# Three schedule edits in an attention and mixture-of-experts kernel: a weight load in pieces, conversions in set rounds, one step of the output normalisation a round later

## The chip, the cores and the metric

One Trainium2 chip, one of its cores. The time is device microseconds from launch to end, the median of the runs. The core has a matrix engine (TensorE, PE in the rows; PEld is its weight load), a vector engine (VectorE, DVE), a scalar engine (ScalarE, ACT), a general engine (GpSimd, POOL) and a queue engine (SyncE, SP) that issues the DMAs here. The five run side by side and wait on each other's semaphores; each runs its own instructions in the order in which the program issued them.

## What is computed

```python
def _attn_ref(q, k, v, centroids):           # batch 2, 8 heads, 768 rows, head_dim 64, 16 clusters
    q_assign = argmax(q_n @ c_n.T); k_assign = argmax(k_n @ c_n.T)      # nearest centroid of each row
    scores = scale * q @ k.T
    scores = where(q_assign[:, None] == k_assign[None, :], scores, -1e9)
    attn = exp(scores - max(scores)); attn /= attn.sum() + 1e-9
    return attn @ v
def _moe_ref(x, w_in, w_out):                # x 1536 x 512, w_in 512 x 2048, both weights float64
    r = maximum(x @ w_in, 0.0); return (r * r) @ w_out
def _moe2_ref(x, domain_probs, w1, w2):      # 4 experts, w1 512 x 1024, w2 1024 x 512
    return sum_e p[:, e:e+1] * (maximum(x @ w1[e], 0) @ w2[e])
```

The first mixture takes the attention's output, the second takes the first one's. Products are made from a high and a low half of each operand in the fast 32-bit matrix format.

## The kernel before

**Attention (to about 268 us).** The 16 heads of both batches are taken two at a time: pair j holds heads 2j and 2j+1. A head has six query tiles of 128 rows, so there are NU = 96 tiles and the loop at line 1094 has 96 rounds, g = 0 to 95. Twelve rounds make a pair; I call g modulo 12 the *turn*. Round g issues, in the order of letters in ORDER (one list for even, one for odd g):

- S: score products of tile g+2 (line 580: two products with q1 and k1, then two with q2 and k2, whose lower rows hold the cluster's one-hot code and so the mask), M: its row maximum on DVE (line 589), E: exp of tile g+1 on ACT (line 600);
- T0, T1: transposes of tile g's exponentials (line 613), with a high copy on ACT (H, line 618) and a low rest on DVE (L, line 619); P0, P1: the product with v (lines 627, 629); O: the copy of a finished output block (line 651);
- X1, X2: at most two *slots*, extra PE jobs taken from `slots` and from `nq`, whose evacuations follow at Y1, Y2; R: what is listed in `early` for this round (DMAs, split of v); C: one entry of the list `dq` of small operations; K: one step of a weight conversion (`convert`).

So even rounds run "S T0 X1 M E T1 R Y1 H0 P0 X2 C H1 L0 L1 C K Y2" and odd ones "S X1 E M T0 T1 Y1 H0 C P1 X2 R L0 H1 C L1 O K Y2 C".

**A pair's preparation** (for j > 1 at turns 10 to 7 ahead of its first tile): four transposes `trans_slot` (line 354; ACT copy, then two POOL operations, lines 52 and 363), two `pair_scores` (line 404), two `pair_turn` (line 420, with DVE sums at line 425). The second `pair_turn` empties `dq` and starts the *cluster chain* `pair_ops`: a DVE maximum (459), three POOL operations (449 to 451), four empty entries, a second DVE maximum (460), four POOL operations (454 to 457). In the eight entries the two maxima and the two POOL groups are m1, p1, four Nones, m2, p2; two are issued at once and the rest one for each C. Then `pair_hot` (line 471) transposes the codes, ACT copies them (476), and `hot_rows` issues four small DMAs (488) into rows D to D+C of q2 and k2, which the second half of S needs. `stack` issues the DMAs of q1, k1, q2, k2 (375, 377). The first pair of this kind, j = 1, has its own rounds in START: transposes in rounds 0, 0, 1, 1, `pair_scores` twice in round 3, `pair_turn` twice in round 4, `pair_hot` in round 7.

**Normalising a pair's output** (`norm_slots`): the list `nq` is filled when a pair's last output block is copied (turn 1) and gives one entry for each following round. f1 (turn 2) puts four small DVE operations at the head of `dq` (lines 670 to 673); f2 (turn 5) transposes the reciprocal sums (679) and, in its evacuation, copies them on ACT (683) and adds the output halves with two POOL additions (688); f3 (turns 8 and 9) spreads them (696), multiplies and splits (702 to 716).

**Weights.** Those of the first mixture are float64, loaded as raw words into `raw` (two buffers, `rawp`). `load_w` at line 111 loads half a part in one DMA of 1 MB. Part 0 of chunk 0 (`raw_t[0, 0, half]`) is loaded ahead of the loop (first half) and in round 4 (second half, line 1082). A column block is converted by `split64`: f1, f2, f4, f5, f6 on DVE (lines 160 to 176) in one scratch buffer `cva`, then f3: an ACT copy (182) and a POOL subtraction (184) that reads `cva` again. The four blocks make 24 steps in `cq`; `convert` takes one in every round from 8 on in which `dq` is empty. When `cq` is empty, `load_piece` loads the next weights in rounds with g % 6 = 4, two pieces each.

**The mixtures (268 us to the end)** are PE products with their evacuations (lines 738 to 920). The change doesn't touch them.

Of the kernel before, what the change touches and what calls it, by code (L numbers as in the profile page):

```python
# [8 lines left out]
F32 = mybir.dt.float32  # L9
F32R = mybir.dt.float32r  # L10
I32 = mybir.dt.int32
# [15 lines left out]
WARM = [12, 10, 5, 11, 3, 9]  # L27
START = {'t': [0, 0, 1, 1], 'a': [3, 3, 4, 4, 7], 'stack1': 4, 'stack': 5, 'head': 2, 'gap': 3}
AT = {"gap": 4, "stack1": -11, "stack": -9, "ohd": -7, "splitv": -3, "load": -8,
      "t": [-14, -13, -12, -11], "a": [-10, -10, -9, -8, -5], "conv": 8}  # L30


@with_exitstack
def moe_attention_kernel(
# [13 lines left out]
    nc = tc.nc  # L48

    def round_pool(dst, src):  # L50

        nc.gpsimd.tensor_scalar(dst, src, 1.0, 1.0, op0=ALU.mult, op1=ALU.mult)
# [5 lines left out]
    NTT = S // 128  # L58
    KD = DM // 128
    TB = 512  # L60
    NTB = NT // TB
    FC = 512
# [9 lines left out]
    rawp = ctx.enter_context(tc.tile_pool(name="raw", bufs=2))  # L72
# [25 lines left out]
    wi32 = moe_w_in.bitcast(I32).rearrange("(k p) f -> p k f", p=128)  # L98
    wo32 = moe_w_out.bitcast(I32).rearrange("(k p) f -> p k f", p=128)
    raw_t = {}  # L100
# [10 lines left out]
    def load_w(ci, part, half):  # L111
        r = rawp.tile([128, 2048], F32, tag="raw", name="raw")
        raw_t[ci, part, half] = r
        r = r.bitcast(I32)
        if part == 0:
            f0 = 2 * (ci * FC + half * FC // 2)
            nc.sync.dma_start(
                out=r.rearrange("p (k f) -> p k f", k=KD), in_=wi32[:, :, f0:f0 + FC])
        else:
            f0 = ci * NF + half * NF // 2  # L120
            nc.sync.dma_start(
                out=r.rearrange("p (k f) -> p k f", k=NF // 2), in_=wo32[:, f0:f0 + NF // 2])

    def w_loads(ci):
        return [(ci, part, half) for part in range(2) for half in range(2)]
# [73 lines left out]
    with tc.manual_schedule():  # L199
# [87 lines left out]
        dq = []  # L287
# [57 lines left out]
        def trans_slot(j, nm, half):  # L345

            def f():
                if half == 0:
                    kq[j, nm] = [kq_p.tile([128, S], F32R, tag=nm + x, name=nm + x) for x in "hl"]
                hs = slice(half * HALF, (half + 1) * HALF)  # L350
                hi, lo = kq[j, nm][0][:, hs], kq[j, nm][1][:, hs]
                m = ps_m.tile([128, HALF], F32, tag="m", name="m")
                for t in range(QT):
                    nc.tensor.transpose(
                        m[:, t * 128:(t + 1) * 128],
                        nat["p", j, nm][:, half * QT + t].rearrange("p e d -> p (e d)"), identf)
                mul = scale if nm == "nq" else 1.0

                def evac():
                    x = kq_p.tile([128, HALF], F32, tag="kqf", name="kqf", bufs=3)  # L360
                    nc.scalar.activation(x, m, AF.Copy, scale=mul)
                    round_pool(hi, x)
                    nc.gpsimd.tensor_tensor(lo, x, hi.bitcast(F32), op=ALU.subtract)
                return evac
            return f
# [198 lines left out]
                        m.rearrange("p t n -> p (t n)").bitcast(F32))  # L564

        def pair_slots(j):
            return [trans_slot(j, nm, half) for nm in ("nk", "nq") for half in range(2)]


        late = []  # L570
# [91 lines left out]
        def norm_slots(hp, last=False):  # L662
            st = {}
            def f1():
                sm = sums_t.pop(hp)
                r = sm_p.tile([128, 2, NTT], F32, tag="r", name="r", bufs=1)
                rs = st["rs"] = sm_p.tile([128, NTT, 2, 2], F32R, tag="rs", name="rs", bufs=2)
                rv = r.rearrange("p h t -> p t h")
                dq[:0] = [
                    lambda: nc.vector.tensor_scalar(r, sm, 1e-9, None, op0=ALU.add),  # L670
                    lambda: nc.vector.reciprocal(r, r),
                    lambda: nc.vector.tensor_copy(rs[:, :, :, 0], rv),
                    lambda: nc.vector.tensor_tensor(
                        rs[:, :, :, 1], rv, rs[:, :, :, 0].bitcast(F32), op=ALU.subtract),
                ]

            def f2():
                m = ps_m.tile([NTT * 4, 128], F32R, tag="m", name="m")
                nc.tensor.transpose(m, st["rs"].rearrange("p t h s -> p (t h s)"), identr)

                def evac():
                    rt = st["rt"] = xs_p.tile([NTT * 4, 128], F32R, tag="rt", name="rt")
                    nc.scalar.copy(rt, m.bitcast(F32))
                    if hp in xm_t:
                        xm = xm_t.pop(hp)
                        for c0 in range(0, S, HALF):
                            cs = slice(c0, c0 + HALF)
                            nc.gpsimd.tensor_tensor(  # L688
                                xs_t[hp][:, cs], xs_t[hp][:, cs], xm[:, cs], op=ALU.add)
                return evac  # L690

            def f3(half):
                b, kt = divmod(hp, H // 2)
                m = ps_m.tile([128, HALF], F32, tag="m", name="m")
                for j in range(QT):
                    nc.tensor.matmul(
                        m[:, j * 128:(j + 1) * 128], sel[:, half * QT + j], st["rt"],
                        start=True, stop=True)

                def evac():  # L700
                    rb = xs_p.tile([128, HALF], F32, tag="rb", name="rb")
                    nc.scalar.copy(rb, m)
                    (nc.vector if last else nc.gpsimd).tensor_tensor(
                        rb, rb, xs_t[hp][:, half * HALF:(half + 1) * HALF], op=ALU.mult)
                    c0 = b * S + half * HALF
                    col = c0
                    while col < c0 + HALF:
                        tb, o = divmod(col, TB)
                        n = min(TB - o, c0 + HALF - col)
                        xn = rb[:, col - c0:col - c0 + n]  # L710
                        hi = xh[tb][:, kt, o:o + n]
                        if last:
                            nc.scalar.copy(hi, xn)
                        else:
                            round_pool(hi, xn)
                        (nc.vector if last else nc.gpsimd).tensor_tensor(
                            xl[tb][:, kt, o:o + n], xn, hi.bitcast(F32), op=ALU.subtract)
                        col += n
                return evac

            if last:
                return [f1, f2, lambda: f3(0), lambda: f3(1)]
            return [f1, None, None, f2, None, None, lambda: f3(0), lambda: f3(1)]


        mp = {}
# [206 lines left out]
        for ci in range(NC1):  # L933
            base = 0 if ci == 0 else NF + 2 if ci == 1 else (ci - 1) * per + 2
            for ci, part, half in w_loads(ci):
                if ci == 0 and part == 0:
                    continue
                js = range(2 * half, 2 * half + 2)
                slot = base + (0 if ci == 0 else NF * part)
                if ci > 0:  # L940
                    plan.append((freed[-2], 1, lambda x=(ci, part, half): load_w(*x)))
                for j in js:
                    plan += split_plan(ci, part, j, slot + j)
                freed.append(slot + js[-1] + 1)
# [89 lines left out]
        for e in range(2):  # L1034
            r = slice(D * e, D * e + D)
# [12 lines left out]
        for _ in range(2):  # L1048
            dq.pop(0)()
        nc.sync.dma_start(out=dp, in_=domain_probs.rearrange("(b p t) e -> p b t e", b=B, t=NTT))  # L1050
        load_w(*w_loads(0)[0])


        early, slots = {}, {}

        def at(d, g, f):
            d.setdefault(max(g, 0), []).append(f)
# [11 lines left out]
        for j in range(1, NH // 2):  # L1069
# [9 lines left out]
            if j + 1 < NH // 2:  # L1079
                at(early, u0 + AT["load"], lambda j=j: load_pair(j + 1))  # L1080
        at(slots, START["head"], onehot_slot(1))
        at(early, 4, lambda: load_w(*w_loads(0)[1]))
        cq, lq = [], []
        for j in range(NF):
            cq += [f for fs in split64(0, 0, j, cv_p[0]) for f in fs]
# [2 lines left out]
        nq = []  # L1088
# [5 lines left out]
        for g in range(NU):  # L1094
            par = g % 2
            todo = slots.pop(g, [])
            if nq:
                f = nq.pop(0)
# [28 lines left out]

            def convert():
                if g >= AT["conv"] and cq:
                    if not dq:  # L1130
                        cq.pop(0)()
                elif not cq and g % NTT == 4:
                    for _ in range(2):
                        lq and lq.pop(0)()
# [48 lines left out]

        hp, pr = NH // 2 - 1, NU // 2 - 1
        f1, f2, f3, f4 = norm_slots(hp, last=True)
        f1()
        while dq:
# [64 lines left out]
        for n in range(NN):  # L1252
# [5 lines left out]
            if n:  # L1258
                fills = [[lambda t=t: token_tile(n - 1, t)] for t in range(NTT)] + [[]]
                order = (1, 5, 6, 2, 7, 4, 3)  # L1260
            else:
                fills = [fill[0:1], fill[1:3], fill[3:4], fill[4:5], fill[5:6], fill[6:7], fill[7:8]]
                order = (1, 2, 5, 6, 7, 4, 3)
            for x, i in enumerate(order):
# [35 lines left out]
                if swap:  # L1300
                    r = PROD[i][1]
# [36 lines left out]
```

## Time and profile before

| | |
|---|---|
| runs | 1042.37, 1042.57, 1043.54 us; median 1042.57 us |
| the profiled execution | 1041.03 us, of which 1039.2 us from its first to its last instruction |
| PE busy | 1023.1 us (98%), granted clock 0.998 in the mean |
| DVE, ACT, POOL busy | 677.9, 537.5, 566.0 us |
| attention loop, from the third tile's scores to the last | 19.8 to 268.7 us |

How to read it: with PE at 98% the busy share hides what is lost, because an operation's modelled end includes what it waited for in the pipe. The starts of the score products are a better clock: one group for each round, and twelve rounds for a pair.

### The profile page before, as it was taken

The page shows a single profiled execution, that of the slowest core. Times are in us where ns is not written, and L with a number is a line of the kernel's source. Part 1 is how long each engine was busy: PE and PEld are TensorE (multiplying, and loading weights), DVE is VectorE, ACT ScalarE, POOL GpSimd, SP SyncE. Part 2 cuts the span into 40 slices and gives each one's busy share as a digit, 9 for nine tenths or more (in the row PEclk, how much of TensorE's full clock was granted, in tenths as well). Part 3 has the DMA queues.
Part 4 walks back from the last instruction along what each step waited for, and adds up shares of the span by engine and source line. Part 5 has one row for each costly group of instructions (what it writes and reads, how often), then busy time and mean ns, then how long its engine had stood idle before and what let it go on. Part 6 is the DMA issues. An engine that isn't in the chain of part 4 may idle for free.

```text
span 1039.2 us, 14949 instructions
## 1 busy us (share of the span) xinstructions
PE 1023.1 (98%) x5549; PEld 907.3 (87%) x5549; DVE 677.9 (65%) x1061; ACT 537.5 (52%) x1080; POOL 566.0 (54%) x557
## 2 busy tenths in 40 slices
PE   8899999999999999999999999999999999999998
PEld 7798999999888888888888998998988888898997
DVE  8788888888687773741175555567776555555654
ACT  6788888888755443434443333433444333333331
POOL 4456866674322222235456566567678566576650
PEclk9999999999999999999999999999999999999999
DMA  4755577652023230221012122122123121121101
GB/s 119 179 134 121 130 187 177 148 126 69 1 82 122 82 110 13 81 82 41 1 42 80 43 81 75 47 81 72 51 81 123 60 82 59 63 82 55 67 1 61
DMA packets 72408, 86.05 MB, mean 83 GB/s; under 512 B 26896, under 2 KB 49744, under 8 KB 72336
## 3 DMA queue, kind: packets, MB, share of 16 engines
q1 hardware_dynamic: 72336, 85.11, 28.6%
q8 instruction: 43, 0.70, 0.3%
q14 instruction: 29, 0.24, 0.1%
HBM read 59.83 MB, written 3.15 MB: 61 GB/s over the span
## 4 chain that ended last, share of the span: by engine, by line
PE 85%; DVE 6%; POOL 5%; DMA 1%; issue 1%; ACT 1%; SPq 0%; POOLq 0%; DVEq 0%; ACTq 0%
PE bank L910 25%; PE bank L870 22%; PE bank L763 13%; PE bank L739 4%; PE bank L740 4%; PE bank L738 4%; PE s L580 3%; PE t L613 3%; PE po L627 2%; PE po L629 2%; DVE nb L589 1%; DVE ptl L619 1%; POOL xs L688 1%; DMA k<-nkh 1%; PE m L404 1%
## 5 line engine op out<-in xcount | busy, mean ns | idle before, releaser
L910 PE MATMUL bank<-w1h,ga 128*128 128x512 f32 x768 | 269.9, 393 | 0.0
L920 DVE SCALAR_TENSOR_TENSOR x<-bank,pe_p,x 128x512 f32<-128x512 f32 x180 | 134.9, 751 | 167.7 <-PE bank L910 167.7
L870 PE MATMUL bank<-xa,w0h 128*128 128x384 f32 x896 | 228.3, 335 | 0.1
L870 PEld LDWEIGHTS bank<-xa,w0h 128*128 128x128 f32 x896 | 164.5, 188 | 17.9 <-ACT fa L881 0.5
L910 PEld LDWEIGHTS bank<-w1h,ga 128*128 128x128 f32 x768 | 144.1, 188 | 24.5
L749 POOL TENSOR_TENSOR ga<-fa,ga 128x512 fp32r<-128x512 f32 x48 | 63.3, 1318 | 175.4 <-ACT ga L748 134.7
L910 PE MATMUL bank<-w1l,ga 128*128 128x512 f32 x384 | 151.6, 395 | 0.0
L870 PE MATMUL bank<-xa,w0l 128*128 128x384 f32 x448 | 149.7, 334 | 0.0
L881 ACT COPY fa<-bank 128x384 f32<-128x384 f32 x96 | 45.5, 474 | 171.6 <-PE bank L870 171.6
L763 PE MATMUL bank<-ga,w1h 128*128 128x512 f32 x384 | 126.6, 389 | 0.0
L890 ACT ACTIVATE ga<-fa 128x384 fp32r<-128x384 f32 x96 | 50.5, 526 | 135.6 <-DVE fa L884 135.6
L839 POOL TENSOR_TENSOR w0l<-raw,w0h 128x512 fp32r<-128x512 f32 x64 | 75.0, 1195 | 81.4 <-ACT w0h L838 81.4
L857 POOL TENSOR_TENSOR w1l<-raw,w1h 128x1024 fp32r<-128x1024 f32 x32 | 77.2, 2414 | 71.3 <-ACT w1h L856 71.3
L619 DVE TENSOR_TENSOR ptl<-t,pth 128x384 fp32r<-128x384 f32 x192 | 97.9, 548 | 27.4 <-ACT pth L618 27.1
L589 DVE TENSOR_REDUCE nb<-s 128x1 f32<-128x768 f32 x96 | 91.4, 952 | 14.8 <-PE s L580 13.8
L893 DVE SCALAR_TENSOR_TENSOR ga<-fa,ga 128x384 fp32r<-128x384 f32 x96 | 90.2, 939 | 0.6 <-ACT ga L890 0.6
L613 PE MATMUL t<-identf,p 128*128 128x128 f32 x576 | 87.7, 277 | 2.8 <-DVE ptl L619 1.9
L600 ACT ACTIVATE p<-s,nb 128x768 f32<-128x768 f32 x96 | 87.7, 913 | 3.8 <-DVE nb L589 3.3
L618 ACT CAST pth<-t 128x384 fp32r<-128x384 f32 x192 | 84.1, 486 | 9.4 <-PE t L613 8.5
L580 PE MATMUL s<-k,q 80*128 80x384 f32 (+1 forms) x384 | 85.3, 343 | 3.7 <-DMA q<-ohm 2.6
L746 ACT ACTIVATE fa<-bank 128x512 f32<-128x512 f32 x44 | 26.3, 597 | 116.4 <-PE bank L740 116.4
L763 PEld LDWEIGHTS bank<-ga,w1h 128*128 128x128 f32 x384 | 72.1, 188 | 14.8
(208 smaller groups left out, 2070.5 us busy)
## 6 DMA issues: line engine op xcount, KB each, us to landing
raw<-in_moe_w_dram SPq DMA_DIRECT2D x64, 512.0 KB, 4.2
raw<-in_moe_w_in_dram SPq DMA_DIRECT2D x8, 1024.0 KB, 5.2
raw<-in_moe_w_out_dram SPq DMA_DIRECT2D x6, 1024.0 KB, 4.9
k<-nkh SPq DMA_DIRECT2D x28, 192.0 KB, 3.3
q<-nqh SPq DMA_DIRECT2D x28, 192.0 KB, 3.0
nv<-in_v_dram SPq DMA_DIRECT2D x16, 192.0 KB, 3.8
out_dram<-x SPq DMA_DIRECT2D x12, 256.0 KB, 2.1
k<-nkl SPq DMA_DIRECT2D x14, 192.0 KB, 4.0
```

What stands on the lines that cost most here:

```text
L580: nc.tensor.matmul(s[:, j, 0:HALF], stk[i, nq][:, t * 128:(t + 1) * 128], stk[i, nk][:, j * HALF:(j + 1) * HALF], start=first, stop=not first)
L589: nc.vector.tensor_reduce(out=nb, in_=s_ps[u][:, :, 0:HALF], axis=AX.XY, op=ALU.max, negate=True)
L600: nc.scalar.activation(p, s_ps.pop(u)[:, :, 0:HALF], AF.Exp, bias=nb_t.pop(u), accum_out=sums_t[hp][:, i % 2, t:t + 1])
L613: nc.tensor.transpose(tp[:, j], p_sb[u][:, half, j * 128:(j + 1) * 128], identf)
L618: return (lambda: nc.scalar.copy(dh, tp), lambda: nc.vector.tensor_tensor(dl, tp, dh.bitcast(F32), op=ALU.subtract))
L619: lambda: nc.vector.tensor_tensor(dl, tp, dh.bitcast(F32), op=ALU.subtract))
L763: nc.tensor.matmul(o, a, b, start=(ft == 0 and z == 0), stop=(ft == NF - 1 and z == 2))
L857: nc.gpsimd.tensor_tensor(lo, w, hi.bitcast(F32), op=ALU.subtract)
L870: nc.tensor.matmul(ps, w[:, o:o + 128], r_op(r, x)[:, kt], start=(first and kt == 0 and z == 0), stop=(kt == 1 and z == 2), skip_group_che ...
L893: nc.vector.scalar_tensor_tensor(out=g_t(n, f, t, 1), in0=h_src(n, f, t), scalar=0.0, in1=g_t(n, f, t, 0).bitcast(F32), op0=ALU.max, op1=A ...
L910: nc.tensor.matmul(o, a, w[:, f], start=(f == 0 and z == 0), stop=(f == 1 and z == 2))
L920: nc.vector.scalar_tensor_tensor(out=acc, in0=o, scalar=pc, in1=acc, op0=ALU.mult, op1=ALU.add)
```

## The change

The 1 MB load of round 4 becomes four DMAs of 256 KB (one for each 128 rows of w_in) in rounds 12 to 15. `convert` works only in turns 2, 6, 7, 8, 9, 10. For pair 1 the transposes go in the order k, q, k, q (first halves first). The last of the four small operations of `norm_slots` (line 673) moves from DVE to POOL, except for the last pair, and f2 comes one round later; f3 keeps its rounds.

```diff
-      "t": [-14, -13, -12, -11], "a": [-10, -10, -9, -8, -5], "conv": 8}
+      "t": [-14, -13, -12, -11], "a": [-10, -10, -9, -8, -5], "conv": 8, "turns": (2, 6, 7, 8, 9, 10)}
...
+    def load_in(kk):
+
+        if kk == 0:
+            raw_t[0, 0, 1] = rawp.tile([128, 2048], F32, tag="raw", name="raw")
+        r = raw_t[0, 0, 1].bitcast(I32).rearrange("p (k f) -> p k f", k=KD)
+        nc.sync.dma_start(out=r[:, kk], in_=wi32[:, kk, FC:2 * FC])
...
         def pair_slots(j):
-            return [trans_slot(j, nm, half) for nm in ("nk", "nq") for half in range(2)]
+            order = [("nk", 0), ("nk", 1), ("nq", 0), ("nq", 1)]
+            if j == 1:
+                order[1:3] = order[2:0:-1]
+            return [trans_slot(j, nm, half) for nm, half in order]
...
                     lambda: nc.vector.tensor_copy(rs[:, :, :, 0], rv),
-                    lambda: nc.vector.tensor_tensor(
+                    lambda: (nc.vector if last else nc.gpsimd).tensor_tensor(
                         rs[:, :, :, 1], rv, rs[:, :, :, 0].bitcast(F32), op=ALU.subtract),
...
-            return [f1, None, None, f2, None, None, lambda: f3(0), lambda: f3(1)]
+            return [f1, None, None, None, f2, None, lambda: f3(0), lambda: f3(1)]
...
-        at(early, 4, lambda: load_w(*w_loads(0)[1]))
+        for kk in range(KD):
+            at(early, 2 * NTT + kk, lambda kk=kk: load_in(kk))
...
                 if g >= AT["conv"] and cq:
-                    if not dq:
+                    if not dq and g % (2 * NTT) in AT["turns"]:
                         cq.pop(0)()
```

## Rows read from the trace of the kernel before

**Rows 1.** The page, part 4: shares of the chain that ended last, by engine

```profile
PE 85%; DVE 6%; POOL 5%; DMA 1%; issue 1%; ACT 1%; SPq 0%; POOLq 0%; DVEq 0%; ACTq 0%
```

**Rows 2.** Windows: stretch, busy of PE, PEld, DVE, ACT, POOL, clock, DMA, GB/s

```profile
50.00:75.00 25.00, 24.85 (x176) 23.52 (x176) 21.51 (x40) 20.32 (x48) 13.87 (x17) 0.93 0.65 147
...
300.00:1039.00 739.00, 735.26 (x3531) 643.61 (x3529) 430.84 (x616) 297.35 (x531) 396.23 (x303) 1.00 0.19 66
```

**Rows 3.** Timeline of PE, round 10: start, us, line, [idle before <- releaser]

```profile
46.56 0.59 PE L580 MATMUL s<-k,q 128*128 128x384 f32 x2 [0.93 <-DMA q<-nqh]
49.75 0.60 PE L580 MATMUL s<-k,q 80*128 80x384 f32 x2 [2.60 <-DMA q<-ohm]
...
51.38 0.42 PE L629 MATMUL po<-ptl,vv 128*128 128x256 f32 x1
```

**Rows 4.** The chain that ended last, in order of time: start, us, what

```profile
37.49 9.61 DMA k<-nkh
47.12 2.62 DMA q<-ohm
```

**Rows 5.** Waits of SP: line, releaser, us in total, times, longest

```profile
SPq L488 <- DMA raw<-in_moe_w_in_dram: 2.6, 1, 2.6
```

**Rows 6.** Timeline of SP and ACT, rounds 4 and 7

```profile
34.78 0.78 SPq L117 DMA_DIRECT2D raw<-in_moe_w_in_dram  x1
...
41.45 0.48 ACT L476 CAST ohm<-m 128x384 fp32r<-128x384 f32 x1
...
44.65 0.66 SPq L488 DMA_DIRECT2D q<-ohm  x1
```

**Rows 7.** Timeline of POOL and PE, rounds 2 and 3

```profile
26.32 1.02 POOL L363 TENSOR_TENSOR nkl<-kqf,nkh 128x384 fp32r<-128x384 f32 x1
...
28.96 0.44 PE L404 MATMUL m<-nql,cp 128*128 128x384 f32 x1 [0.56 <-POOL nql L363]
...
29.46 1.01 POOL L363 TENSOR_TENSOR nql<-kqf,nqh 128x384 fp32r<-128x384 f32 x1
```

**Rows 8.** Timeline of PE: score products that open rounds 22, 34, 46 and 58

```profile
82.28 0.86 PE L580 MATMUL s<-k,q 128*128 128x384 f32 x4
...
115.75 0.86 PE L580 MATMUL s<-k,q 128*128 128x384 f32 x4
...
147.12 0.86 PE L580 MATMUL s<-k,q 128*128 128x384 f32 x4
...
177.98 0.86 PE L580 MATMUL s<-k,q 128*128 128x384 f32 x4
```

**Rows 9.** Timeline of DVE, round 23: a conversion's first step

```profile
90.02 0.72 DVE L160 TENSOR_SCALAR cva<-raw 128x512 int32<-128x512 int32 x1 [1.67 <-POOL w0l L184]
```

**Rows 10.** Timeline of DVE, POOL and PE, rounds 30 and 31 (turns 6 and 7)

```profile
107.99 1.00 DVE L176 SCALAR_TENSOR_TENSOR cva<-raw,cva 128x512 int32<-128x512 int32 x1
...
108.53 0.67 POOL L455 TENSOR_SCALAR oh<-A 128x192 fp32r<-128x192 f32 x1
...
109.99 0.45 PE L471 MATMUL m<-identr,oh 128*128 128x128 f32 x3 [0.53 <-POOL oh L457]
...
110.48 1.28 POOL L184 TENSOR_TENSOR w0l<-cva,w0h 128x512 fp32r<-128x512 f32 x1 [0.54 <-ACT w0h L182]
```

**Rows 11.** Timeline of DVE, POOL and PE, rounds 52 to 55, without conversions

```profile
164.98 0.16 DVE L673 TENSOR_TENSOR rs<-r,rs 128x12 fp32r<-128x12 f32 x1
...
168.22 1.99 POOL L688 TENSOR_TENSOR xs<-xs,xm 128x384 f32<-128x384 f32 x2
...
171.10 0.35 POOL L455 TENSOR_SCALAR oh<-A 128x192 fp32r<-128x192 f32 x1
...
172.24 0.45 PE L471 MATMUL m<-identr,oh 128*128 128x128 f32 x3 [0.21 <-POOL oh L457]
```

**Rows 12.** DMA issues from 0 to 280 us: count, KB each, median us to landing

```profile
raw<-in_moe_w_in_dram SPq DMA_DIRECT2D x2, 1024.0 KB, 7.6
raw<-in_moe_w_out_dram SPq DMA_DIRECT2D x8, 256.0 KB, 4.6
```

## The prediction

> **What bounds the kernel now.** I read the chain that ended last first: it is PE for 85% of the span, with small links of DVE and POOL [rows 1]. Then the windows: from 300 us on PE is busy 735.3 of 739.0 us [rows 2], so what the change saves ahead of that is handed on to the end in full, and nothing can be saved there. What is left is the attention loop, and there busy shares say little. So I took the timeline of PE and read the start of the score products of each round. Twelve rounds make a pair. The starts that open turn 10 stand at 46.56, 82.28, 115.75, 147.12 and 177.98 us [rows 3, 8]. Their differences are 35.72, 33.47, 31.37 and 30.86 us; the fourth pair has no conversions and no weight load of the old round 4, so it is the yardstick. The first three exceed it by 4.86, 2.61 and 0.51 us, 7.98 in all; another 0.93 us is the wait just ahead of 46.56 [rows 3]. These 8.91 us are what there is to win from the load and the conversions; the reader should see that they lie in the first 150 us.
>
> **The stall of round 10.** The scores of head 2's first tile wait 0.93 us for q1 and then 2.60 us for the one-hot rows [rows 3]. Why: the chain goes from a DMA of k that took 9.61 us, issued just behind the 1 MB load, to the issue of the last one-hot DMA, which then takes 2.62 us [rows 4]. The codes were copied by 41.45 + 0.48 = 41.93 us, but the first of their four DMAs issued at 44.65 [rows 6]; SP waited 2.6 us of this for the 1 MB load itself [rows 5]. So the load issued at 34.78 holds them twice, by its bytes and because the queue's ninth DMA waits for its first. After the wait PE runs slow: a product with v takes 0.42 us at 51.38 [rows 3], and the granted clock of 50 to 75 us is 0.93 in the mean [rows 2], that is some 1.75 us lost (0.07 x 25), where PE ran at the lower of its two levels, 1.2 GHz.
>
> **Part 1, load in pieces in rounds 12 to 15.** It takes the load out of that place. The four one-hot DMAs then issue from 41.93 on, 0.66 us apart [rows 6]: the last at about 43.9, landed 2.62 later at 46.5. PE would start the first half of the scores at 46.56 - 0.93 = 45.63 and the second 0.59 later, at 46.2. So a wait of at least 0.3 us stays; I take 0.6, since PE's ends are modelled, and 2.6 (nothing won but the clock) as the far bound. With so short a gap I expect no fall of the clock. Four issues on SP instead of one cost nothing: nothing late is queued behind them there. The pieces land in some 4.6 us each like their kin [rows 12] and are first read by block 2's f1, about round 32.
>
> Here a page speaks against the change: the Trainium skill's "DMA: Bandwidth & Descriptors", section "Bandwidth", advises batches of 1 MiB or more and gives smaller ones a lower rate. The rows agree in direction: four times 4.6 us against 7.6 for the whole [rows 12].
>
> **Part 2, conversions in six turns.** Steps that used to come in nine turns of a pair now come in turns 2 (f5), 6 (f6), 7 (f3), 8 (f1), 9 (f2), 10 (f4); the first block starts at 8, 9, 10. So four pairs have one block each, where before two and a half pairs did. What goes: f1 in round 23, in front of a full POOL queue, where DVE stood 1.67 us for the scratch buffer that POOL was still to read [rows 9]; with its echo that is most of pair 2's 2.61 us. What stays is known, since the third block went through just these turns: f6 in round 30 ran beside the cluster chain, line 455 took 0.67 us there against 0.35 without a conversion, and PE waited 0.53 us for the chain against 0.21 [rows 10, 11]. That is 0.32, say 0.33 us a pair, now in four pairs: 1.3 us. f5 in turn 2 stands ahead of the DVE operations that lead to the chain's first maximum; no row prices that, so I take 0 and, as the other bound, 0.3 a pair (a third of line 176's 1.00, its kin). f1 in turn 8 follows f3 by one round: in round 31 line 184 ran at 110.48 to 111.76 [rows 10], early in the round that ends with f1, so the buffer is free in time. The later `load_piece` rounds (58 to 76 for 40 to 58) cost nothing; their data is wanted after round 95.
>
> Parts 1 and 2 together: of 8.91 us there remain 0.6 + 1.3, so **7.0 us** are won (bounds 3.5 and 8.5).
>
> The Trainium skill's "SBUF — State Buffer", section "Who interferes with whom", says that a DVE instruction with two SBUF inputs and a GpSimd instruction that reads SBUF exclude each other for the whole instruction. The 0.67 against 0.35 agrees with a partial meeting; by a full one each pair would lose more (a rival, below).
>
> **Part 3, order of pair 1's transposes.** In round 3 the first `pair_scores` waited 0.56 us for the low half of q [rows 7]. With k, q, k, q that operation takes the place of the one that ends at 26.32 + 1.02 = 27.34, so this wait goes. The second `pair_scores` still needs POOL's last operation, which ends at 30.47 [rows 7] as before; PE gets there about 0.8 us sooner and now waits for it some 0.2. Won: **0.6 us** (0 to 0.85), and the codes of pair 1 come as much sooner.
>
> **Part 4, normalisation.** Line 673 leaves DVE just ahead of the chain's first maximum: 0.16 us long [rows 11], about 0.12 from its start to the maximum's. PE waits 0.21 us at line 471 [rows 11], so it gets that back in the six pairs whose chain runs beside a normalisation: **0.7 us** (0 to 1.0). POOL does it while it waits for that maximum, at no cost.
>
> f2 a round later is meant to put the two additions of line 688, 1.99 us on POOL ahead of the chain's second group [rows 11], behind it. I count through the letters. `pair_turn` evacuates in turn 4 and issues two of the eight entries; turn 4 has two C behind that, turn 5 three: four Nones and m2. p2 comes at turn 6's first C. f2, now in X1 of turn 6, evacuates at Y1, and in even rounds Y1 stands before the first C. POOL's order stays p1, additions, p2. So I take **0** for this edit; the PE transpose that moves (one matmul) shifts a little work from turn 5 to turn 6, under the wait at 471.
>
> **Sum.** 7.0 + 0.6 + 0.7 = 8.3 us. The profiled execution took 1041.03 us, 1.54 less than the median of the runs, 1042.57; I take the saving off both: 1032.7 profiled, **1034.3** for the median.
>
> **Rivals.**
> 1. *The pieces crowd the next pair.* They land between the DMAs of heads 3 and 4, and round 16 or 22 stalls as round 10 did. Price: round 10's, 0.93 + 4.86 less about 0.4 for conversions, 5.4 us: 1039.7. For it: they take more transfer time in sum [rows 12]. Against: those heads' DMAs have several rounds to land. 8%. The page on DMA points this way.
> 2. *f6 blocks the chain in full.* In four pairs the chain loses the whole 1.00 us of line 176 [rows 10] and not 0.33: 4 x 0.67 = 2.7 us more, 1037.0. 10%; the SBUF page's rule in its strongest form.
> 3. *f2 does move the additions.* If p2 comes first, PE's waits at 471 vanish: 1.3 us of part 2 and some 0.5 more, 1032.5. 8%, since the count of letters says otherwise.
> 4. *Slower: f1 held by POOL.* f1 in turn 8 needs the buffer that line 184 reads. If line 184 (1.28 us, [rows 10]) fell behind POOL work as long as the additions (1.99 [rows 11]), DVE would stand about 3 us in rounds 20, 32 and 44, and PE about 0.4 more each as in round 23 (1.67 on DVE, some 2.06 on PE): 3 x 3.4 = 10.2 us, 1044.5. It decides from about 2.8 us of standing a time. Against: the order at 110.48 [rows 10]. 5%.
> 5. Mixtures of 1 and 2 that leave nothing measurable: 3%.
>
> **How the numbers follow.** The forecast has 66%, and its own range is 1031.8 (all bounds at their best) to 1037. For 8 in 10 the range must reach over rivals 2 and 3 and the far bound of the stall: 1031.8 to 1039.0. A measurement can tell about 0.2%, 2.1 us, from no change. Faster by that: 66 + 10 + 8 and half of rival 1, 88%. Within it: the other half and the mixtures, 7%. Slower: rival 4, 5%.
>
> **What would show it.** After: round 10's scores with one short wait and a clock of 1.00 from 50 to 75 us; pair lengths from turn 10 to turn 10 of about 31.2 in the first four pairs and 30.75 later; no DVE wait at line 160; line 404 without its 0.56; line 688 still ahead of 454, and the wait at 471 near 0.1 without a conversion and 0.4 with one. I am wrong if the one-hot rows still land late, if DVE waits at line 160, or if pairs 1 to 4 stay above 32.

## The result and the profile after

The changed kernel takes **1033.01 us** (median; 1032.07 to 1033.69), the kernel before beside it 1042.47; ratio 0.9912, 95% interval 0.9892 to 0.9933. The forecast was 1034.3, in a range of 1031.8 to 1039.0. A second comparison on another chip gave 1032.97 against 1040.77, ratio 0.9922 (0.9908 to 0.9935); two single runs of all that follow, 1253.92 and 3323.28 us, were disturbed and are left out. The kernel before spreads more (1037.91 to 1043.54 over all comparisons) than the changed one (1032.07 to 1034.01): what went was partly a stall whose length, and the lower clock behind it, change from run to run ("Part 1" below).

The profiled execution spans 1030.2 us, 9.0 less than before. The chain's shares and the windows that answer to [rows 1, 2]:

```profile
PE 89%; DVE 5%; POOL 5%; issue 1%; ACT 1%; POOLq 0%; DVEq 0%; ACTq 0%
```

```profile
50.00:75.00 25.00, 24.30 (x182) 22.69 (x181) 21.76 (x39) 21.65 (x52) 16.31 (x23) 1.00 0.71 178
300.00:1030.00 730.00, 726.09 (x3490) 636.03 (x3488) 423.94 (x607) 289.51 (x517) 392.48 (x300) 1.00 0.19 65
```

The DMA link is gone from the chain, the clock of 50 to 75 us is 1.00 for 0.93, and the mixtures are as full as they were. The score products that open turn 10, in the timeline of PE of the changed kernel, answer to [rows 3, 8]:

```profile
44.44 0.86 PE L590 MATMUL s<-k,q 128*128 128x384 f32 x4
...
75.64 0.86 PE L590 MATMUL s<-k,q 128*128 128x384 f32 x4
...
107.01 0.86 PE L590 MATMUL s<-k,q 128*128 128x384 f32 x4
...
138.21 0.86 PE L590 MATMUL s<-k,q 128*128 128x384 f32 x4
...
169.43 0.86 PE L590 MATMUL s<-k,q 128*128 128x384 f32 x4
```

Round 10's four products now run in one go, with no wait in front of them or between them. The pairs take 31.20, 31.37, 31.20 and 31.22 us where they took 35.72, 33.47, 31.37 and 30.86.

**Where the time went, round by round.** The table gives round lengths, from one start of score products to the next, in the profiled executions: before, changed, and three of the experiments below. Rounds not listed agree within 0.1 us before and after the change, and within 0.22 in the others.

| rounds (turn) | before | changed | load alone (run 1) | turns alone (run 2) | additions behind (run 11) |
|---|---|---|---|---|---|
| start of the first scores | 16.17 | 15.61 | 16.07 | 15.76 | 15.92 |
| 3 | 4.31 | 3.83 | 4.32 | 4.32 | 3.82 |
| 9 to 11 | 12.45 | 6.88 | 6.89 | 13.54 | 6.95 |
| 14 (2) | 3.76 | 3.49 | 3.55 | 3.49 | 3.50 |
| 19 (7) | 2.78 | 2.98 | 2.78 | 3.06 | 2.30 |
| 24 to 26 (0 to 2) | 10.57 | 8.47 | 10.58 | 8.32 | 8.48 |
| 31 (7) | 3.05 | 2.98 | 3.05 | 3.04 | 2.31 |
| 37, 38 (1, 2) | 6.34 | 5.90 | 6.35 | 5.90 | 5.90 |
| 43 and 55 (7) | 2.73, 2.72 | 2.98, 2.99 | 2.72, 2.72 | 3.06, 3.05 | 2.30, 2.30 |
| 67 and 79 (7) | 2.72, 2.72 | 2.66, 2.67 | 2.72, 2.72 | 2.72, 2.72 | 2.31, 2.30 |
| 88 (4) | 2.78 | 2.07 | 2.87 | 2.77 | 2.08 |

So of the 9.0 us, 5.57 are round 10's stall, 1.9 the conversions (rounds 14, 24 to 26, 31, 37 and 38, less what rounds 19, 43 and 55 and their neighbours pay), 0.48 is round 3, 0.71 round 88, and 0.56 lies ahead of the first scores; some 0.2 is lost again in many small pieces, most of it behind the last scores. The start of the first scores differs between executions of like code (15.6 to 17.7 in the runs below), so the 0.56 isn't the change's.

### The profile page after: what moved, and what is told of

Same layout as the page of the kernel before. It is cut to its first block, busy times and chain, and to the rows that moved or that the text cites. A ratio compares the mean times of both kernels' runs of the same rounds, so it can differ in the third digit from the quotient of the medians.

```text
span 1030.2 us, 14964 instructions
## 1 busy us (share of the span) xinstructions
PE 1019.0 (99%) x5549; PEld 906.1 (88%) x5549; DVE 675.2 (66%) x1054; ACT 536.3 (52%) x1080; POOL 568.2 (55%) x564
## 4 chain that ended last, share of the span: by engine, by line
PE 89%; DVE 5%; POOL 5%; issue 1%; ACT 1%; POOLq 0%; DVEq 0%; ACTq 0%
PE bank L920 25%; PE bank L880 22%; PE bank L773 13%; PE s L590 4%; PE t L623 4%; PE bank L750 4%; PE bank L748 4%; PE bank L749 4%; PE po L637 2%; PE po L639 2%; POOL xs L698 1%; DVE ptl L629 1%; DVE nb L599 1%; PE m L361 1%; PE m L706 1%
## 5 line engine op out<-in xcount | busy, mean ns | idle before, releaser
L900 ACT ACTIVATE ga<-fa 128x384 fp32r<-128x384 f32 x96 | 50.5, 526 | 135.5 <-DVE fa L894 135.5
L628 ACT CAST pth<-t 128x384 fp32r<-128x384 f32 x192 | 83.6, 485 | 11.5 <-PE t L623 10.4
```

The lines of the kernel that those rows point to most:

```text
L628: return (lambda: nc.scalar.copy(dh, tp), lambda: nc.vector.tensor_tensor(dl, tp, dh.bitcast(F32), op=ALU.subtract))
```

## The experiments

Short diffs; the first two and the ninth start from the kernel before, the others from the changed kernel.

**1. The load alone.**

```diff
-        at(early, 4, lambda: load_w(*w_loads(0)[1]))
+        for kk in range(KD):
+            at(early, 2 * NTT + kk, lambda kk=kk: load_in(kk))
```

> The kernel before with the load alone changed: four pieces in rounds 12 to 15, all else as it was. If the stall of round 10 is the load's alone, rounds 9 to 11 lose 5.5 to 5.6 us against before (3.16, 5.89 and 3.40 us become 2.07, 2.40 and 2.41), while round 3 stays at 4.31 and rounds 24 to 26 at 2.6, 4.0 and 4.0: about 1037 us in the median. The rival, that the calmer conversions had a share in it, says that a wait of over 0.5 us stays in round 10.

Measured: 1035.68 us (1035.62 to 1036.04) against 1040.80, ratio 0.9953 (0.9939 to 0.9968). Rounds 9 to 11 take 6.89 us; rounds 14 and 17 change by about 0.2, all other rounds stay within 0.15. By the ratio the load is worth 4.9 us by itself.

**2. The six turns alone.**

```diff
-                    if not dq:
+                    if not dq and g % (2 * NTT) in AT["turns"]:
```

> The kernel before with the six turns alone. My theory of conversions: rounds 24 to 26 fall by 2.1 us in sum, rounds 37 and 38 by 0.4, round 14 by 0.25, and round 7 of each of the first four pairs (19, 31, 43, 55) stands at 3.0 us, so some 2 us less than before; the stall of rounds 9 to 11 stays at 12.4 us in sum. About 1040.5 us. The rival, that the conversions only mattered because the stall had put DVE behind, says that 24 to 26 keep over 1 us of their excess.

Measured: 1038.65 us (1036.35 to 1039.98) against 1040.80, ratio 0.9983 (0.9970 to 0.9997): 1.8 us by the ratio. Rounds 24 to 26 come down to 8.32 and the chain's rounds of turn 7 cost about 3.05 in four pairs, but the stall of round 10 stays whole; it is even longer here, with a granted clock of 0.89 from 50 to 75 us. Its scores, in the timeline of PE:

```profile
45.96 0.59 PE L580 MATMUL s<-k,q 128*128 128x384 f32 x2 [0.70 <-DMA q<-nqh]
49.09 0.98 PE L580 MATMUL s<-k,q 80*128 80x384 f32 x2 [2.54 <-DMA q<-ohm]
```

Load and turns thus act apart: 4.9 + 1.8 + 0.48 (round 3) + 0.71 (round 88) is 7.9 us, beside 8.1 by the ratio of the second comparison and 9.2 by that of the first, where the kernel before ran longer. Each ratio's interval is about 3 us wide, so a small interplay of the two would not show.

**3. The late load as one DMA of 1 MB** in round 12.

```diff
-        for kk in range(KD):
-            at(early, 2 * NTT + kk, lambda kk=kk: load_in(kk))
+        at(early, 2 * NTT, lambda: load_w(*w_loads(0)[1]))
```

> The changed kernel with the same 1 MB in one DMA in round 12 instead of four pieces in rounds 12 to 15. If what counts is only that the load is later, every round keeps its length within 0.1 us. If the pieces matter, the DMAs of heads 3 and 4 issued just behind it land late and one of rounds 16 or 22 waits 1 us or more.

Measured: 1033.18 us, one execution. Rounds 9 to 22 are those of the changed kernel within 0.03 us; rounds 46 and 48 are 0.28 and 0.38 longer, which also occurs in runs 5 and 6, whose load is in pieces. The pieces themselves bring nothing that this can tell; the later place does.

**4. Four pieces, but in round 4.**

```diff
-            at(early, 2 * NTT + kk, lambda kk=kk: load_in(kk))
+            at(early, 4, lambda kk=kk: load_in(kk))
```

> The changed kernel with its four pieces issued in round 4, where the whole load stood. If the bytes ahead of the one-hot rows make the stall, rounds 9 to 11 are back near 12 us in sum (7 in the changed kernel). If it was the one long DMA that the queue waited for when it came to its ninth, the pieces, which land sooner, leave less than half of the 5.6 us.

Measured: 1041.72 us, one execution. Its first scores come 2.07 us later than the changed kernel's, with a granted clock of 0.93 in the first 25 us (1.00 there), which isn't the edit's doing. Rounds 9 to 11 take 13.75 us: the stall is back in full. Timelines of SP and PE:

```profile
36.14 4.03 SPq L129 DMA_DIRECT2D raw<-in_moe_w_in_dram  x4
...
46.08 0.66 SPq L495 DMA_DIRECT2D q<-ohm  x1
```

```profile
47.39 0.58 PE L590 MATMUL s<-k,q 128*128 128x384 f32 x2 [0.72 <-DMA q<-nqh]
51.25 0.98 PE L590 MATMUL s<-k,q 80*128 80x384 f32 x2 [3.27 <-DMA q<-ohm]
```

SP no longer waits for a load at the one-hot issue (the 2.6 us of [rows 5] have no counterpart), so that wait is not what the stall needs. What it needs is seen in the landings. These are the DMA views, narrowed to the 192 KB transfer just ahead of the one-hot rows and to the first one-hot DMA, with the us from issue to landing last: the kernel before (issued at 41.48 and 44.65), this run (45.43 and 46.08) and the changed kernel (40.46 and 41.02).

```profile
xm<-xs SPq DMA_DIRECT2D x1, 192.0 KB, 7.5
q<-ohm SPq DMA_DIRECT2D x1, 24.0 KB, 4.5
...
xm<-xs SPq DMA_DIRECT2D x1, 192.0 KB, 5.1
q<-ohm SPq DMA_DIRECT2D x1, 24.0 KB, 4.6
...
xm<-xs SPq DMA_DIRECT2D x1, 192.0 KB, 3.4
q<-ohm SPq DMA_DIRECT2D x1, 24.0 KB, 3.0
```

In all three the one-hot rows land some 0.2 us behind that transfer (49.0 and 49.15, 50.5 and 50.7, 43.9 and 44.0), whether they were issued 3.2 us after it or 0.6. So it is the transfers queued ahead that make the stall, and by these landings SP's wait in the kernel before did not lengthen it. SP's own time adds a smaller part here. Of the 4.03 us that the four issues take, one waits 2.5, which the view of waits puts down to PE; the DMA engines were 0.36 busy for 1.5 us of that time, and 0.91 in the 11.5 us behind it. By these shares about 1 us was lost (an estimate). Waits of SP, and the window (its DMA share is the last but one number):

```profile
SPq L129 <- PE t L623: 2.5, 1, 2.5
```

```profile
38.20:39.70 1.50, 1.50 (x13) 1.34 (x13) 1.50 (x3) 1.50 (x5) 1.00 (x1) 1.00 0.36 84
```

**5. The additions really behind the chain:** they go to the end of `dq`, behind p2.

```diff
-                        xm = xm_t.pop(hp)
-                        for c0 in range(0, S, HALF):
...
+                        def adds(xm=xm_t.pop(hp)):
+                            for c0 in range(0, S, HALF):
...
+                        dq.append(adds)
```

> The changed kernel with line 698's two additions put at the end of dq, so that they are issued at the second C of turn 6, behind the chain's second POOL group. If the additions ahead of that group are what PE still waits for at the one-hot transposes, round 7 of a pair falls from 2.98 to about 2.5 us in the first four pairs and from 2.66 to about 2.5 in the later ones: some 2.2 us in sum, about 1031 us. The rival, that the chain is bound by its maxima on DVE and not by POOL, leaves round 7 where it is.

Measured: 1030.42 us (1029.32 to 1030.89) against 1040.51, ratio 0.9897 (0.9877 to 0.9916). Turn 7 falls to 2.30 us in all six pairs; turn 8 pays 0.11 where there is a conversion.

**6. Line 683 (the old 673) back on DVE.**

```diff
-                    lambda: (nc.vector if last else nc.gpsimd).tensor_tensor(
+                    lambda: nc.vector.tensor_tensor(
```

> The changed kernel with the fourth small operation of the normalisation back on DVE. By the prediction's step rounds 5 to 7 of six pairs grow by 0.12 us in sum each, 0.7 us in all, and round 88 stays at 2.07. By the theory after the result (the maximum behind it waits for its own input anyway) rounds 5 to 7 stay, and round 88, where it would meet the additions on POOL, stays too, because the additions now come a round later: nothing is lost at all.

Measured: 1034.34 us, one execution. Turns 5 to 7 of the six pairs don't change (at most 0.03), as expected; but round 88 takes 2.85 us for 2.07, and that I had not expected ("Part 4" below). Rounds 10 and 46 are 0.37 us longer each, with a wait for one-hot rows, and round 48 by 0.33, where the transposes wait for DVE (line 629); these differ from run to run.

**7. f2 back in its old round.**

```diff
-            return [f1, None, None, None, f2, None, lambda: f3(0), lambda: f3(1)]
+            return [f1, None, None, f2, None, None, lambda: f3(0), lambda: f3(1)]
```

> The changed kernel with f2 back in turn 5, the fourth small operation staying on POOL. If the 0.71 us of round 88 came from that operation on DVE meeting the additions, round 88 stays at 2.07; if it came from the additions' place, it is back at 2.8. Rounds 5 to 7 of the late pairs: 2.60, 2.07, 2.72 as in the kernel before, the same sum as 2.59, 2.13, 2.66.

Measured: 1032.22 us, one execution, within the changed kernel's spread. Turn 6 takes 2.07 for 2.14 and turn 7 3.04 for 2.98 (2.73 for 2.66 without a conversion): a shift of 0.07 that cancels. Round 88 stays at 2.07.

**8. Turn 6 without a conversion step, turn 11 with one.**

```diff
-"turns": (2, 6, 7, 8, 9, 10)}
+"turns": (2, 7, 8, 9, 10, 11)}
```

> The changed kernel with conversions in turns 2, 7, 8, 9, 10, 11, so that no step with two SBUF inputs runs on DVE while the chain's second POOL group does. If f6 in turn 6 is what lengthens round 7 by 0.3 us in the first four pairs, it falls there from 2.98 to 2.66 (1.3 us in sum) and turn 2 or 11 pays under 0.1. The rival, that f3's copy on ACT in turn 7 lengthens it, leaves it at 2.98.

Measured: 1031.77 us, one execution. Turn 7 takes 2.66 us in all pairs (2.98 before with a conversion); rounds 37 and 49 grow from 2.41 to 2.59, more than the 0.1 I had allowed, so that pairs 1 to 4 take 31.02 to 31.07 for 31.20 to 31.37. In the timeline of POOL and PE, line 462 is back at 0.35 us and the transposes of the codes don't wait:

```profile
131.13 0.35 POOL L462 TENSOR_SCALAR oh<-A 128x192 fp32r<-128x192 f32 x1
...
132.28 0.45 PE L478 MATMUL m<-identr,oh 128*128 128x128 f32 x3
```

**9. The load alone, and no conversion step in round 23.**

```diff
-                    if not dq:
+                    if not dq and g != 23:
```

> The kernel before with the load in pieces in rounds 12 to 15, and one conversion step less: none in round 23, where DVE stood 1.67 us for the scratch buffer; every later step comes one round later. If that single wait made pair 2's excess, rounds 24 to 26 (2.61, 4.00, 3.97 with the load alone moved) fall to about 2.4, 2.4 to 2.6 and 3.5 to 3.75, some 2 us less. The rival, that nine conversions in a pair are too many wherever they stand, leaves over 1 us of the excess in rounds 24 to 29.

Measured: 1034.95 us, one execution (load alone: 1035.68). DVE no longer stands at the conversion's first step. Timelines of DVE, of the load alone and of this kernel:

```profile
84.52 0.73 DVE L167 TENSOR_SCALAR cva<-raw 128x512 int32<-128x512 int32 x1 [1.66 <-POOL w0l L191]
```

```profile
84.84 1.10 DVE L167 TENSOR_SCALAR cva<-raw 128x512 int32<-128x512 int32 x1
```

Score products of this kernel, rounds 24 to 27, in the timeline of PE:

```profile
81.17 0.87 PE L587 MATMUL s<-k,q 128*128 128x384 f32 x4
83.79 0.86 PE L587 MATMUL s<-k,q 128*128 128x384 f32 x4
86.19 0.87 PE L587 MATMUL s<-k,q 128*128 128x384 f32 x4
90.15 0.88 PE L587 MATMUL s<-k,q 128*128 128x384 f32 x4
```

Round 25 falls from 4.00 to 2.40 us, but 24 stays at 2.62 and 26 at 3.96. The wait was worth 1.6 us of pair 2's excess of 2.61, less than the 2 I expected. The other 1.0 stays: rounds 24 (0.2) and 26 (0.47) are longer than with the six turns, which put no step into turns 0 and 1, and round 31 (0.3) has f6 beside the chain. The shifted steps made pair 3 longer (32.20 for 31.35).

**10 and 11. The changed kernel again, and the additions behind again,** on one chip.

> The changed kernel once more, beside the next one on the same chip: 7 to 9 us less than the kernel before, ratio 0.991 to 0.993; its times spread less than those of the kernel before, whose stall in round 10 varies.

> The changed kernel with the additions behind the chain's second POOL group: 3.0 us less than the changed kernel by the rounds of its profile (four pairs with round 7 at 2.30 for 2.98 and round 8 at 2.89 for 2.78, two pairs with 2.30 for 2.66), so 0.3% less in the median. The rival, that round 10's waits take it back, leaves under 1 us.

Measured, against 1040.77 us before: 1032.97 (1032.29 to 1034.01), ratio 0.9922 (0.9908 to 0.9935), and 1030.61 (1029.62 to 1030.73), ratio 0.9899 (0.9883 to 0.9914). The additions behind p2 beat the changed kernel by 2.4 us, where I expected 3.0; the two ranges don't touch, and this is the best of the kernels run. Their timeline of POOL and PE:

```profile
189.43 0.84 POOL L461 TENSOR_TENSOR A<-A,mx 128x384 f32<-128x384 f32 x1 [0.67 <-DVE mx L467]
...
191.52 1.98 POOL L698 TENSOR_TENSOR xs<-xs,xm 128x384 f32<-128x384 f32 x2
...
192.44 0.38 PE L478 MATMUL m<-identr,oh 128*128 128x128 f32 x3
```

POOL now waits 0.67 us for the second maximum and starts the chain's second group at once; the additions follow, and PE doesn't wait.

## Why the prediction was right or wrong, point by point

**Part 1 held, with one term mis-sized and one cause too many.** The timelines of ACT and SP of the changed kernel answer to [rows 6]:

```profile
40.43 0.48 ACT L483 CAST ohm<-m 128x384 fp32r<-128x384 f32 x1
```

```profile
41.02 0.66 SPq L495 DMA_DIRECT2D q<-ohm  x1
...
43.05 0.59 SPq L495 DMA_DIRECT2D q<-ohm  x1
```

The first one-hot DMA issues 0.11 us after the copy's end (40.91), for 2.72 before, and the last 2.03 later, as the 0.66 each said. The term that was off is the landing: I carried over 2.62 us [rows 4], measured behind a stream of other transfers, and for the wrong DMA. The first tile needs only three of the four: `hot_rows` issues even blocks of q2, both halves of k2, then odd blocks of q2, which are the next tile's. The third, issued at 42.42, landed 1.9 us later, before PE opened the scores at 44.44. The DMA view, narrowed to it:

```profile
k<-ohm SPq DMA_DIRECT2D x1, 24.0 KB, 1.9
```

Hence no wait, for 0.6 predicted. In other runs of this load place round 10 was 0 to 0.37 us longer, so 0.6 is a bound rather than a value. Nor did the load hold the rows twice: the wait for it [rows 5] is there, but run 4 and the landings show that it was off the path, and the bytes alone held them. For the whole stall the sum had 0.93 + 4.86, less 0.4 for conversions and 0.6 for the wait: 4.8; rounds 9 to 11 gave 5.57, and the load alone 4.9.

The clock of 1.00 came as said, and it weighs more than its place in the text suggests. From 50 to 75 us the granted clock was 0.93 before, 0.89 in run 2 and 0.87 in run 4, wherever the stall stood in a trace. It doesn't always fall: of the 14 runs of the kernel before beside runs 1 to 4, two have a mean clock of 1.000 and took 1037.91 and 1037.98 us, the other twelve, at 0.996 to 0.998, took 1039.66 to 1042.87. The load alone (1035.68) saves 2.3 us against those two and 5.1 against the median. So about half of what the load gives back goes with the lower clock; whether the wait was also shorter in those two runs, no trace shows.

The Trainium skill's "DMA: Bandwidth & Descriptors", section "Bandwidth", asks for batches of 1 MiB or more. Run 3 obeys it and is the changed kernel's equal (1033.18 against 1033.01): where the data is wanted many rounds later (a first read about round 32, as the prediction has it), the rate decides nothing.

**Part 2 held.** Its share of the 7.0 was 7.0 - 4.8 = 2.2; the rounds gave 1.9 and the turns alone 1.8. The price of f6 beside the chain was to be 0.33 us a pair. The changed kernel's timeline of DVE, POOL and PE, a pair with a conversion and one without, answers to [rows 10, 11]:

```profile
99.34 0.89 DVE L183 SCALAR_TENSOR_TENSOR cva<-raw,cva 128x512 int32<-128x512 int32 x1
99.77 0.67 POOL L462 TENSOR_SCALAR oh<-A 128x192 fp32r<-128x192 f32 x1
...
101.24 0.45 PE L478 MATMUL m<-identr,oh 128*128 128x128 f32 x3 [0.47 <-POOL oh L464]
```

```profile
193.40 0.35 POOL L462 TENSOR_SCALAR oh<-A 128x192 fp32r<-128x192 f32 x1
...
225.42 0.45 PE L478 MATMUL m<-identr,oh 128*128 128x128 f32 x3 [0.16 <-POOL oh L464]
```

0.67 against 0.35 is the 0.32 again, four times over; turn 7 takes 2.98 with and 2.66 without, and run 8 shows that the step in turn 6 is the cause. Rival 2 (the whole of line 183) didn't come. Of pair 2's excess run 9 gives DVE's wait 1.6 of 2.6 us: most of it, as argued, but 1.0 has other causes. Rival 4 didn't come: the changed kernel's waits of DVE have no row for line 167. Nor did rival 1: rounds 16 and 22 are as short as before.

**Part 3 held:** 0.48 us for 0.6. Round 3 takes 3.80 to 3.84 us in every run with the new order and 4.27 to 4.32 in every run without it. The wait of 0.56 [rows 7] is gone, and a gap of about 0.2 stands ahead of the second `pair_scores`' last product, as the text had it. The changed kernel's timeline of PE, the last two products of the second:

```profile
29.60 0.34 PE L411 MATMUL m<-nqh,cp 128*128 128x384 f32 x1
30.01 0.44 PE L411 MATMUL m<-nql,cp 128*128 128x384 f32 x1
```

**Part 4 failed in its place and came back by chance elsewhere.** The step "about 0.12 from its start to the maximum's ... PE gets that back in the six pairs" gave nothing: run 6 puts line 683 back and turns 5 to 7 stay, and the pairs behind the fourth take 30.87 us, as before, for 30.75 forecast. Two timelines of DVE, before and changed:

```profile
195.38 0.55 DVE L425 TENSOR_REDUCE A<-m 128x192 f32<-128x384 f32 x1
195.84 0.16 DVE L673 TENSOR_TENSOR rs<-r,rs 128x12 fp32r<-128x12 f32 x1
195.96 0.55 DVE L459 TENSOR_REDUCE mx<-A 128x24 f32<-128x384 f32 x1
```

```profile
186.82 0.55 DVE L432 TENSOR_REDUCE A<-m 128x192 f32<-128x384 f32 x1
187.41 0.55 DVE L466 TENSOR_REDUCE mx<-A 128x24 f32<-128x384 f32 x1
```

From the sums (line 425, now 432) to the maximum that reads them it is 0.58 us with the small operation between and 0.59 without. The maximum can't start before the sums are there; line 673 ran in a gap that exists anyway. I had read the distance between two starts as a cost without asking what else the later one waited for.

The 0.71 us of round 88 I had not foreseen. There the additions don't wait behind a chain (the last pair has none) and start when their DMA lands, just as line 673 runs. POOL, DVE and PE before:

```profile
252.19 1.96 POOL L688 TENSOR_TENSOR xs<-xs,xm 128x384 f32<-128x384 f32 x2 [2.35 <-DMA xm<-xo]
252.36 0.86 DVE L673 TENSOR_TENSOR rs<-r,rs 128x12 fp32r<-128x12 f32 x1
...
253.75 0.55 PE L613 MATMUL t<-identf,p 128*128 128x128 f32 x3 [0.44 <-DVE ptl L619]
```

and run 6, with the operation put back on DVE:

```profile
245.20 1.96 POOL L698 TENSOR_TENSOR xs<-xs,xm 128x384 f32<-128x384 f32 x2 [2.44 <-DMA xs<-xo]
245.29 0.94 DVE L683 TENSOR_TENSOR rs<-r,rs 128x12 fp32r<-128x12 f32 x1
...
246.75 0.55 PE L623 MATMUL t<-identf,p 128*128 128x128 f32 x3 [0.51 <-DVE ptl L629]
```

An operation on 128 x 12 elements takes 0.86 and 0.94 us beside the additions, for 0.16 alone, and `ptl`, and PE, wait behind it. In the changed kernel it takes 0.23 on POOL and runs ahead of the additions:

```profile
243.52 0.23 POOL L683 TENSOR_TENSOR rs<-r,rs 128x12 fp32r<-128x12 f32 x1 [2.22 <-DMA xm<-xo]
243.72 1.97 POOL L698 TENSOR_TENSOR xs<-xs,xm 128x384 f32<-128x384 f32 x2
```

Run 7, where only f2 goes back, keeps the gain, so it is line 673's and not f2's. The Trainium skill's "SBUF — State Buffer", section "Who interferes with whom", names this pair: a DVE instruction with two SBUF inputs and a GpSimd instruction that reads SBUF lock each other out. The rows agree, for one of the two additions. The 0.7 of the sum was thus the right size for a wrong reason, and the total owes that to luck.

**f2 a round later: 0, as counted.** The changed kernel's timeline of POOL shows the order that the letters gave, p1, additions, p2:

```profile
190.54 1.97 POOL L698 TENSOR_TENSOR xs<-xs,xm 128x384 f32<-128x384 f32 x2
...
192.47 0.84 POOL L461 TENSOR_TENSOR A<-A,mx 128x384 f32<-128x384 f32 x1
```

Rival 3 says what it would be worth if they changed places: 1.8 us. Run 11, which does that, is 2.4 us faster than run 10, more than the rival's price: without a conversion turn 7 falls by 0.36, where the wait at line 478 was 0.16 at most.

**The sum.** Predicted 8.3; 7.9 by parts and 9.0 in the profiled pair, of which 0.56 lies ahead of the first scores. What stays open: why rounds 10 and 46 wait some tenths for one-hot rows in some executions and not in others, which steps lengthen rounds 24 and 26, and how much of the load's price is the lower clock and how much a longer wait.

## What to carry to other kernels

A stall that ended in a small, late DMA was cured by taking the large one out from ahead of it; whether it then goes in pieces mattered less than when it goes. The distance between two starts on an engine isn't the price of the operation between them: look for what else the later one waits for. Before calling a step moved, count where the instructions behind it are issued; the additions had to go to the end of the list, one round later wasn't enough.

## What the runs showed of the hardware

A vector operation on 128 x 12 elements took 0.86 to 0.94 us while a POOL addition of two SBUF tiles ran, against 0.16 us alone. From one DVE reduction to the next that reads its result, 0.58 us passed for an operation of 0.55, with or without a third one between. The one-hot DMAs of 24 KB landed some 0.2 us behind the 192 KB transfer issued before them, in three kernels; from its own issue the last took 1.9 us with little ahead of it, and 2.62 [rows 4] or 2.84 (run 4's chain) behind a crowd. Four issues of 256 KB in one round took SP 4.03 us, 2.5 of them put down to a wait for PE; one issue of 1 MB took 0.78 [rows 6]. Where PE had waited 2.5 to 3.3 us in round 10, the mean granted clock of 50 to 75 us was 0.87 to 0.93, and 1.00 where the stall was gone.
